# Block transposes on VectorE and a way through DRAM in place of TensorE's transposes, in an LSH attention with an FFN

## The chip, the core and the metric

The program runs on one core of one Trainium2 chip. The metric is the device time of one execution in microseconds. "Before" was run three times. TensorE (PE in the profile, its weight loads PEld), VectorE (DVE), ScalarE (ACT) and GpSimd (POOL) work each through a queue of their own, in order; SyncE (SP) only issues DMAs.

## The reference

```
scores = q @ k.T / sqrt(64)                      # 4 batches, 8 heads, 768 rows, head size 64
scores = where(bucket(q) == bucket(k), scores, -1e9)    # buckets: signs of 6 projections
attn   = softmax(scores);   x = attn @ v         # to 3072 tokens of 512
h = x @ w_in;   g = h * clip(h + 3, 0, 6) / 6;   out = g @ w_out    # 512 -> 2048 -> 512
```

## The kernel before

Attention runs in 192 tiles: 32 heads (4 batches of 8) of six tiles, each 128 queries by 768 keys. Index k or g counts tiles, i heads. Products are float32 in two float32r parts, a rounded high part and a low part (the rest), so every matmul stands two or three times with parts of its operands.

For one tile: `scores` writes the scores (minus sign and bucket penalty included) into PSUM tile s; `lowest` (L340, DVE) copies them to the SBUF tile p and takes the row minimum; `exponential` (L352, ACT) makes p the probabilities, in place, and adds up the row. The values product needs keys on the partitions, and p has queries there; so `transp` (L362) transposes p by TensorE against the identity, six blocks of 128x128 into two PSUM tiles pt of three blocks. `split_p` copies each pt to its high part ph (L385, ACT) and puts the rest into pl (L386, DVE). `values` multiplies two tiles at once, in two halves of three key blocks; `output` (L427) takes the sum to SBUF, and DMAs bring it to a DRAM tile xs, a second part by an adding DMA from POOL.

The FFN (`ffn`) goes through 12 chunks of 256 tokens (three for each batch), 16 steps each. A step is `gemm1` (12 matmuls of 256 columns into h), `gate` (relu L514 on ACT, the product L515 on DVE, high part gh L519, low part gl L520) and, one step later, `gemm2` (six matmuls of 512 columns into po). The chunks of batch 0 run by themselves between tiles 52 and 53 (`first_ffn`). Those of batches 1 to 3 follow the attention by one batch: the generator `fill` is advanced twice a tile, so that from tile 106 on one FFN step stands beside every attention tile. When attention ends, 58 steps are left and run alone.

The order on PE, DVE, ACT and POOL is that of the program text. The main loop's round k issues the transposes of tile k, the exponential of k+1, the minimum of k+2, the scores of k+3 (LA), and the split of k. DMAs on SP are put in order by the framework; SP too works in order, and a DMA that waits holds up those behind it. `lead` also prepares the next head: a load, the cast L275, DMAs of parts, and on POOL scaling and splits (L249, L281, L283), and, once in six tiles, `hash_qk` on TensorE and `bits` (L301) on DVE.

Buffers that matter here: p two, the gate's gh and gl two each, g one, a tag "ob" with two of 4 KB for a chunk's inputs and outputs, pt two under each of two names. GF = 2 * 48 + FS is the tile from which the round takes its FFN form.

## Time and profile before

| what | value |
|---|---|
| median of three runs (range) | 1031.67 us (1030.36 to 1032.12) |
| the profiled execution | 1030.6 us, span 1028.8 us, granted clock 0.999 |
| TensorE busy, 600 to 700 us | 99.63 us of 100 |
| transposes L362 on PE | 1152 instructions |
| L386 pl<-pt,ph on DVE | 376, mean 550 ns |
| L385 ph<-pt on ACT | 376, mean 481 ns |
| DMA | 80.69 MB, mean 78 GB/s |

Busy times of one engine come from the profiler's records; matmuls overlap, so a group's mean is longer than the step from one start to the next. "Idle before" names what the engine waited for last. The chain follows the work that ended last back through what released it. A stretch's row gives the busy time of each engine within it.

### The profile page before, as it was taken

Reading aid. Unit: us, or ns where it says so; the run is one execution under the profiler, and the core shown is the slowest. Engines: PE = TensorE matmul, PEld = TensorE weight load, DVE = VectorE, ACT = ScalarE, POOL = GpSimd, SP = SyncE. Lnnn points to the kernel's source line nnn. Section 1 sums busy time; section 2 is a strip of 40 time slices with the busy share of each in tenths; the row PEclk is TensorE's granted clock in tenths of the full one; section 3 lists DMA queues with packets and bytes.
Section 4 is the critical chain, followed back from the end, with each engine's and each line's share of the span. In section 5 each row is a group of like instructions: output and inputs, shape, how many; then the busy total and the mean of one; then the engine's idle time right before and its main releaser. Section 6 shows DMA issues by size and latency. Waiting matters only on the chain.

```text
span 1028.8 us, 19009 instructions
## 1 busy us (share of the span) xinstructions
PE 1006.9 (98%) x6846; PEld 924.3 (90%) x6846; DVE 687.9 (67%) x1446; ACT 585.3 (57%) x1311; POOL 473.1 (46%) x535
## 2 busy tenths in 40 slices
PE   8999999999999999999999999999999999999997
PEld 7999878888999998898999999999899999899996
DVE  7999988998489998756555666665656553333332
ACT  6889865555488886554645554555454452333332
POOL 6777725666367775544544534543544232200100
PEclk9999999999999999999999999999999999999999
DMA  4567679000145555222321322321231011101000
GB/s 124 139 146 181 155 228 333 2 1 1 41 128 122 114 118 138 64 63 53 100 56 26 85 76 51 76 68 38 63 101 38 20 32 29 42 1 42 1 22 20
DMA packets 47413, 80.69 MB, mean 78 GB/s; under 512 B 5924, under 2 KB 27812, under 8 KB 47320
## 3 DMA queue, kind: packets, MB, share of 16 engines
q1 hardware_dynamic: 42840, 73.98, 24.8%
q0 software_dynamic: 4480, 5.51, 4.8%
q8 instruction: 54, 0.88, 0.4%
q14 instruction: 39, 0.32, 0.1%
HBM read 41.95 MB, written 18.09 MB: 58 GB/s over the span
## 4 chain that ended last, share of the span: by engine, by line
PE 80%; DVE 11%; ACT 4%; issue 3%; POOL 1%; DMA 1%; SPq 0%; DVEq 0%; POOLq 0%; ACTq 0%
PE pt L362 10%; PE h L506 7%; PE h L505 7%; PE h L507 7%; PE po L527 7%; PE po L529 7%; PE po L528 7%; PE acc L399 6%; PE acc L400 6%; PE s L330 5%; PE s L333 5%; DVE pl L386 2%; DVE p L340 2%; PE z L292 1%; DVE wr L192 1%
## 5 line engine op out<-in xcount | busy, mean ns | idle before, releaser
L340 DVE TENSOR_SCALAR_CACHE_REDUCE p<-s 128x768 f32<-128x768 f32 x192 | 183.4, 955 | 98.8 <-PE pt L362 95.0
L386 DVE TENSOR_TENSOR pl<-pt,ph 128x384 fp32r<-128x384 f32 x376 | 191.7, 550 | 50.2 <-ACT ph L385 48.2
L385 ACT CAST ph<-pt 128x384 fp32r<-128x384 f32 x376 | 165.5, 481 | 53.6 <-PE pt L362 43.1
L352 ACT ACTIVATE p<-p,m 128x768 f32<-128x768 f32 x192 | 179.5, 935 | 7.0 <-DVE p L340 6.5
L514 ACT ACTIVATE g<-h,three 128x256 f32<-128x256 f32 x192 | 91.5, 476 | 152.8 <-PE h L507 131.5
L520 POOL TENSOR_TENSOR gl<-g,gh 128x256 fp32r<-128x256 f32 x96 | 74.3, 774 | 204.2 <-DVE gh L519 160.6
L362 PE MATMUL pt<-ident,p 128*128 128x128 f32 x1152 | 160.4, 273 | 5.2 <-DVE pl L386 3.3
L362 PEld LDWEIGHTS pt<-ident,p 128*128 128x128 f32 x1152 | 135.8, 140 | 23.5 <-PE pt L362 3.9
L515 DVE SCALAR_TENSOR_TENSOR g<-g,h 128x256 f32<-128x256 f32 x192 | 80.5, 420 | 113.8 <-ACT g L514 111.3
L399 PE MATMUL acc<-ph,vv 128*128 128x256 f32 x564 | 152.2, 302 | 4.0 <-DVE pl L386 4.0
L505 PE MATMUL h<-xh,w 128*128 128x256 f32 x512 | 147.7, 289 | 1.2 <-ACT y L427 1.2
L506 PE MATMUL h<-xl,w 128*128 128x256 f32 x512 | 143.3, 280 | 0.4 <-DVE xl L497 0.4
L507 PE MATMUL h<-xh,w 128*128 128x256 f32 x512 | 143.2, 280 | 0.0
L400 PE MATMUL acc<-pl,vv 128*128 128x256 f32 x564 | 140.6, 282 | 0.0
L527 PE MATMUL po<-w,gh 128*128 128x512 f32 x320 | 126.7, 396 | 0.1
L529 PE MATMUL po<-w,gl 128*128 128x512 f32 x320 | 126.6, 396 | 0.0
L528 PE MATMUL po<-w,gh 128*128 128x512 f32 x320 | 126.1, 394 | 0.0
L399 PEld LDWEIGHTS acc<-ph,vv 128*128 128x128 f32 x564 | 107.0, 190 | 7.2 <-DVE pl L386 2.1
L400 PEld LDWEIGHTS acc<-pl,vv 128*128 128x128 f32 x564 | 107.4, 190 | 0.0
L330 PE MATMUL s<-kk,qq 76*128 76x384 f32 x384 | 100.9, 343 | 2.0 <-ACT kk L306 1.5
L505 PEld LDWEIGHTS h<-xh,w 128*128 128x128 f32 x512 | 96.4, 188 | 3.8 <-ACT y L427 2.4
L333 PE MATMUL s<-kk,qq 128*128 128x384 f32 x384 | 99.8, 341 | 0.0
(136 smaller groups left out, 2022.6 us busy)
## 6 DMA issues: line engine op xcount, KB each, us to landing
raw<-in_qkT SPq DMA_DIRECT2D x32, 384.0 KB, 3.5
kk<-qq SPq DMA_DIRECT2D x62, 192.0 KB, 3.2
wr<-in_w_in SPq DMA_DIRECT2D x16, 512.0 KB, 11.1
wr<-in_w_out SPq DMA_DIRECT2D x16, 512.0 KB, 3.9
vr<-in_v SPq DMA_DIRECT2D x32, 192.0 KB, 2.6
qq<-qq SPq DMA_DIRECT2D x31, 192.0 KB, 3.1
out<-ob SPq DMA_DIRECT2D x11, 512.0 KB, 2.7
xr<-xs SPq DMA_DIRECT2D x9, 512.0 KB, 3.7
```

What stands on the lines that cost most here:

```text
L340: nc.vector.tensor_scalar(out=pr_[:], in0=s[:, :, :HW], scalar1=CAP, scalar2=None, op0=ALU.min, op1=ALU.min, accum_out=m[:],)
L352: nc.scalar.activation(pr_[:], pr_[:], AF.Exp, bias=m[:], scale=-1.0, accum_out=sms[b][:, t, h : h + 1])
L362: nc.tensor.transpose(pt[:, x], probs[g][0][:, c, x * P : (x + 1) * P], ident[:])
L386: nc.vector.tensor_sub(lo[:, :, w], pt[:], hi[:, :, w].bitcast(F32))
L399: nc.tensor.matmul(acc[:], lhsT=vv[:, kt], rhs=hi[:, x], start=(kt == 0), stop=False)
L400: nc.tensor.matmul(acc[:], lhsT=vv[:, kt], rhs=lo[:, x], start=False, stop=(kt == KT - 1))
L505: nc.tensor.matmul(hp[:], lhsT=wi[:, 0, wc], rhs=xh, start=(cc == 0), stop=False)
L506: nc.tensor.matmul(hp[:], lhsT=wi[:, 0, wc], rhs=xl, start=False, stop=False)
L507: nc.tensor.matmul(hp[:], lhsT=wi[:, 1, wc], rhs=xh, start=False, stop=(cc == NCC - 1))
L527: nc.tensor.matmul(po[u], lhsT=gh[:, us], rhs=wo[:, 0], start=(fc == 0), stop=False)
L528: nc.tensor.matmul(po[u], lhsT=gh[:, us], rhs=wo[:, 1], start=False, stop=False)
L529: nc.tensor.matmul(po[u], lhsT=gl[:, us], rhs=wo[:, 0], start=False, stop=(fc == NFC - 1))
```

## The change

From tile 106 on (GT = 2 * 48 + FS + FT with FS = 8, FT = 2) TensorE transposes nothing. `flip` transposes p on VectorE, each block of 32x32 for itself, into a tile f, which SP writes to a DRAM tile fd. `move` reads it back in four DMAs of 32 partitions x 4 x 192 numbers each, so that every 32x32 block comes to the partitions of its keys; the two targets (spare and px) take turns. `split_p` reads the target two rounds later (LT = 2). To make the blocks land so, the scores of these tiles take their keys in another order (`half`). The second half's sub goes from DVE to POOL, and the gate's gh beside the FFN from DVE to ACT. A new function `beside_ffn` writes the round from tile 105 on, with 194 rounds in place of 192. Tiles f share the two p buffers. The "ob" buffers become "oa" and "ob", of which "ob" is spare's later; gh and gl become one tile, in "ga" and "gb" in turn, and "gb" alone while px holds "ga". POOL's long instructions for a head come in two halves from head 19 on (`spans`). FS goes from 4 to 8, so the FFN beside attention starts some tiles later.

The diff, without the parts that only rename tiles or hand buffers on:

```
@@ -28,7 +28,9 @@
-FS = 4
+FS = 8
+FT = 2
+LT = 2
...
@@ -216,11 +227,15 @@
     GF = 2 * HK + FS
+    GT = GF + FT
...
@@ -240,7 +255,7 @@
-        n = 4 if i <= 2 else 1
+        n = 4 if i <= 2 else 2 if i > GF // KT + 1 else 1
...
@@ -325,12 +340,17 @@
         k1, k2, q1, q2 = state[i]
         us = slice(t * P, (t + 1) * P)
         s = scs[g] = pair(f"s{g}")
+        def half(x, c: int):
+            if g < GT:
+                return x[:, c * HW : (c + 1) * HW]
+
+            x = x.rearrange("p (x g b) -> p g x b", x=KT, g=4)
+            return x[:, 2 * c : 2 * c + 2]
+
         for c in range(2):
-            cs_ = slice(c * HW, (c + 1) * HW)
-            nc.tensor.matmul(s[:, c, :HW], lhsT=q1[:KM, us], rhs=k1[:KM, cs_], start=True, stop=False)
+            nc.tensor.matmul(s[:, c, :HW], lhsT=q1[:KM, us], rhs=half(k1[:KM], c), start=True, stop=False)
         for c in range(2):
-            cs_ = slice(c * HW, (c + 1) * HW)
-            nc.tensor.matmul(s[:, c, :HW], lhsT=q2[:, us], rhs=k2[:, cs_], start=False, stop=True)
+            nc.tensor.matmul(s[:, c, :HW], lhsT=q2[:, us], rhs=half(k2, c), start=False, stop=True)
 
     def lowest(g: int):
 
...
@@ -362,6 +382,33 @@
             nc.tensor.transpose(pt[:, x], probs[g][0][:, c, x * P : (x + 1) * P], ident[:])
         if c:
             del probs[g]
+
+
+
+    written, moved, homes = {}, {}, []
+
+    def flip(g: int):
+        nonlocal written
+        x = sp.tile([P, S], F32, name=f"f{g}", tag="p", bufs=2)
+        nc.vector.transpose(x[:], probs.pop(g)[0][:].rearrange("p c k -> p (c k)"))
+        d = dp.tile([P, S], F32, name=f"fd{g}", tag="fd", bufs=4)
+        dma(out=d[:], in_=x[:])
+        written[g] = d, last
+
+    def move(g: int):
+        if not homes:
+            px = sp.tile([P, S], F32, name="px", tag="ga", bufs=1)
+            homes.extend([spare[0][:, :S], px[:]])
+        to = moved[g] = homes[g % 2]
+        d, _ = written.pop(g)
+        after = written[g + 1][1] if g + 1 in written else last
+        with tc.issue_after(after.ins):
+            for x in range(4):
+                r = slice(32 * x, 32 * x + 32)
+                dma(
+                    out=to[r].rearrange("b (i c) -> b i c", i=4),
+                    in_=d[:].rearrange("(i b) (g c) -> g b i c", i=4, g=4)[x],
+                )
 
     lent = []
 
...
@@ -380,10 +427,24 @@
                     for x in ("ph", "pl")
                 ]
             parts[u, c] = [x.rearrange("p (x w q) -> p x w q", x=QT, w=2) for x in both]
-        hi, lo = parts[u, c]
-        pt = pts.pop((g, c))
-        nc.scalar.copy(hi[:, :, w], pt[:])
-        nc.vector.tensor_sub(lo[:, :, w], pt[:], hi[:, :, w].bitcast(F32))
+        hi, lo = (x[:, :, w] for x in parts[u, c])
+        engine = nc.vector
+        if g < GT:
+            pt = pts.pop((g, c))[:]
+        else:
+            pt = moved[g].rearrange("p (i x a) -> p x i a", i=4, x=KT)[:, c * QT : (c + 1) * QT]
+            hi, lo = (x.rearrange("p x (i a) -> p x i a", i=4) for x in (hi, lo))
+            if c:
+                engine = nc.gpsimd
+        nc.scalar.copy(hi, pt)
+        lows.append(lambda: engine.tensor_sub(lo, pt, hi.bitcast(F32)))
+
+    lows = []
+
+    def split_lows():
+        for f in lows:
+            f()
+        lows.clear()
 
     accs = {}
     vdone = 0
...
@@ -507,17 +570,28 @@
+    g_turn = 0
+    def gate_tiles(n: str):
+        nonlocal g_turn
+        g_turn += 1
+        if homes or g_turn % 2:
+            x = sp.tile([P, 2, TC], F32R, name=f"gb{n}", tag="gb", bufs=1)
+        else:
+            x = sp.tile([P, 3, TC], F32R, name=f"ga{n}", tag="ga", bufs=1)
+        return x[:, 0], x[:, 1]
     def gate(n: str, fc: int, hp, copy, engine, between=lambda: None):
         g = sp.tile([P, TC], F32, name=f"g{n}_{fc}", tag="g", bufs=1)
-        gh = sp.tile([P, TC], F32R, name=f"gh{n}_{fc}", tag="gh")
-        gl = sp.tile([P, TC], F32R, name=f"gl{n}_{fc}", tag="gl")
+        gh, gl = gate_tiles(f"{n}_{fc}")
         nc.scalar.activation(g[:], hp[:], AF.Relu, bias=three[:], scale=1.0)
         nc.vector.scalar_tensor_tensor(
             out=g[:], in0=g[:], scalar=6.0, in1=hp[:], op0=ALU.min, op1=ALU.mult
         )
         between()
-        copy(gh[:], g[:])
-        engine.tensor_sub(gl[:], g[:], gh[:].bitcast(F32))
+        copy(gh, g[:])
+        engine.tensor_sub(gl, g[:], gh.bitcast(F32))
         return gh, gl
 
     def gemm2(fc: int, po, gh, gl):
...
@@ -804,7 +880,7 @@
-            copy, engine = (nc.scalar.copy, nc.vector) if b == B - 1 else (nc.vector.tensor_copy, nc.gpsimd)
+            copy, engine = nc.scalar.copy, nc.vector if b == B - 1 else nc.gpsimd
...
@@ -892,7 +968,47 @@
             ahead(0, x)
         for _ in range(2):
             cv(0)
-        for k in range(NS):
+        def beside_ffn(k: int):
+
+            for c in range(2):
+                if k < GT:
+                    transp(k, c)
+            whole = False
+            for _ in range(1 if k < GT else 2):
+                u = vnext // 2
+                if u < NS // 2 and (k < GT or k % 2 == 0 and k >= 2 * u + 2 + (LT if 2 * u >= GT else 0)):
+                    whole = value_half()
+            if k + 1 < NS:
+                exponential(k + 1)
+            late = k if k < GT else k - LT
+            if GT <= late < NS or k < GT:
+                for c in range(2):
+                    split_p(late, c, False)
+            next(fill, None)
+            if whole:
+                output(vnext // 2 - 1)
+            if k == NS + LT - 1:
+                homes.clear()
+            if k + 1 < NS:
+                flip(k + 1)
+            if k + 2 < NS:
+                lowest(k + 2)
+            split_lows()
+            if GT <= k < NS:
+                move(k)
+            if k + LA < NS and (k + LA) % KT == 2 and (k + LA) // KT + 1 < NJ:
+                hash_qk((k + LA) // KT + 1)
+                bits((k + LA) // KT + 1)
+            next(fill, None)
+            if k + LA < NS:
+                lead(k + LA)
+            else:
+                add()
+
+        for k in range(NS + LT):
+            if k >= GT - 1:
+                beside_ffn(k)
+                continue
             end = GB if k < GB else NS
             i, t = divmod(k, KT)
             if k == HK - XE:
```

What the change does to the order, at three places. First VectorE in one tile beside the FFN (step 6 of chunk 1), up to the next tile's first row: p is the scores' copy, pl_0 and pl_1 the two low halves, g the gate's product, gh its high part. Before:

```order
L340 TENSOR_SCALAR p_7146,m_7145<-s_7113 128x768
L386 TENSOR_TENSOR pl_0_7182<-pt_0_7136,ph_0_7181 128x3x128
L386 TENSOR_TENSOR pl_1_7186<-pt_1_7140,ph_1_7185 128x3x128
L515 SCALAR_TENSOR_TENSOR g_1_6_7195<-g_1_6_7195,h_1_6_7161 128x256
L519 CAST gh_1_6_7196<-g_1_6_7195 128x256
L340 TENSOR_SCALAR p_7212,m_7211<-s_7176 128x768
```

And now (f is the transposed tile, spare and px the two targets of the moves):

```order
L393 STREAM_TRANSPOSE f_7231<-p_7157 128x768
L360 TENSOR_SCALAR p_7236,m_7235<-s_7191 128x768
L440 TENSOR_TENSOR pl_0_7211<-spare,ph_0_7210 128x3x128
L589 SCALAR_TENSOR_TENSOR g_1_6_7250<-g_1_6_7250,h_1_6_7216 128x256
L393 STREAM_TRANSPOSE f_7279<-p_7236 128x768
```

The second sub and the cast gh are gone from this queue; the block transpose stands ahead of the minimum, behind the product of the step before.

Second, ScalarE at the same place, from one exponential (out p) to the next; y is the values' sum. Before:

```order
L352 ACTIVATE p_7097,sms_5328<-p_7097,m_7096 128x768
L427 COPY y_0_7174<-acc_7148 128x256
L385 CAST ph_0_7181<-pt_0_7136 128x3x128
L385 CAST ph_1_7185<-pt_1_7140 128x3x128
L514 ACTIVATE g_1_6_7195<-h_1_6_7161,three 128x256
L352 ACTIVATE p_7146,sms_5328<-p_7146,m_7145 128x768
```

And now, with gb the gate's one buffer:

```order
L372 ACTIVATE p_7157,sms_5278<-p_7157,m_7156 128x768
L439 CAST ph_0_7210<-spare 128x3x128
L439 CAST ph_1_7213<-spare 128x3x128
L488 COPY y_0_7103<-acc_7196 128x256
L588 ACTIVATE g_1_6_7250<-h_1_6_7216,three 128x256
L593 CAST gb_1_6_7251<-g_1_6_7250 128x256
L372 ACTIVATE p_7236,sms_5278<-p_7236,m_7235 128x768
```

The casts read SBUF instead of PSUM, and the gate's cast has come between the relu and the next exponential.

Third, where the new rounds begin on VectorE: from round 106 to round 109, rt being the transposed reciprocals that scale the first chunk xr.

```order
L529 TENSOR_TENSOR xr_0_5538<-xr_0_5538,rt_0_0_5690 128x256
L393 STREAM_TRANSPOSE f_5697<-p_5657 128x768
L360 TENSOR_SCALAR p_5702,m_5701<-s_5671 128x768
L529 TENSOR_TENSOR xr_0_5538<-xr_0_5538,rt_0_1_5717 128x256
L393 STREAM_TRANSPOSE f_5722<-p_5702 128x768
L360 TENSOR_SCALAR p_5727,m_5726<-s_5711 128x768
L316 TENSOR_SCALAR qq_5662<-z_5733,thr,val 44x768
L529 TENSOR_TENSOR xr_0_5538<-xr_0_5538,rt_0_2_5759 128x256
L393 STREAM_TRANSPOSE f_5764<-p_5727 128x768
L360 TENSOR_SCALAR p_5769,m_5768<-s_5747 128x768
L440 TENSOR_TENSOR pl_0_5754<-spare,ph_0_5753 128x3x128
L529 TENSOR_TENSOR xr_0_5538<-xr_0_5538,rt_0_3_5787 128x256
```

Each of these rounds scales one of the chunk's four parts beside a block transpose and a minimum; the first product of the FFN (L589) stands only behind this piece, in round 110. On SP each tile adds the write of f and four moves. Two tiles of it, with the parts of the next head between:

```order
L78 DMA fd_5699<-f_5697 128x768
L78 DMA spare<-fd_5654 32x4x192 x4
L78 DMA raw_5745<-in_qkT 128x768
L78 DMA fd_5724<-f_5722 128x768
L78 DMA px<-fd_5699 32x4x192 x4
L78 DMA kk_5661<-qq_5662 12x768
L78 DMA vr_5777<-in_v 128x384
L78 DMA fd_5766<-f_5764 128x768
L78 DMA spare<-fd_5724 32x4x192 x4
```

The write of a tile stands ahead of the moves of the tile before it, and the next head's DMAs take their places between.

More of the change, by code (lines that the diff above doesn't have):

```diff
@@ L912, in lsh_attention_moe @@
                 pair_turn = 0
-            third = k < GF + 2
+            third = True
             whole = False
-            for _ in range(1 if third and k != HK else (2, 0)[k % 2]):
+            for _ in range(1 if k != HK else 2):
                 if vnext < k - k % 2:
@@ L940, in lsh_attention_moe @@
                 next(fill, None)
-            if k + LA >= NS:
-                add()
             if k < GB:
```

35 lines of the change are left out of this document (25 added, 10 removed).

## Prediction

> **What bounds the kernel now.** The page comes first: its engine line, and the chain that ended last.
>
> ```profile
> span 1028.8 us, 19009 instructions
> PE 1006.9 (98%) x6846; PEld 924.3 (90%) x6846; DVE 687.9 (67%) x1446; ACT 585.3 (57%) x1311; POOL 473.1 (46%) x535
> PE 80%; DVE 11%; ACT 4%; issue 3%; POOL 1%; DMA 1%; SPq 0%; DVEq 0%; POOLq 0%; ACTq 0%
> ```
>
> TensorE is busy 98% and carries 80% of the chain. An average hides stages, so the second view is the busy time by stretches: first the stage that the change rewrites (attention beside the FFN), then the tail with the FFN alone.
>
> ```profile
> 500.00:600.00 100.00, 99.76 (x687) 92.51 (x686) 61.30 (x130) 53.52 (x122) 48.01 (x48) 1.00 0.29 71
> 900.00:1000.00 100.00, 100.00 (x652) 90.37 (x651) 35.01 (x87) 36.32 (x83) 6.33 (x12) 1.00 0.05 17
> ```
>
> The columns are length, PE, PEld, DVE, ACT, POOL, granted clock, DMA share, GB/s. In both stretches TensorE has no gap and a full clock, so there a TensorE instruction costs what it takes from the next one's start. The third view is the window from the first transpose of tile 106 to the last of tile 191, for the transposes' line alone; then one tile's six transposes in the chain, and two starts of the FFN's second product.
>
> ```profile
> 413.40:851.90 438.50, 70.25 (x516) 61.12 (x516) 1.00 0.25 60
> 413.52 0.49 PE L362 MATMUL pt<-ident,p 128*128 128x128 f32 x3
> 851.27 0.82 PE L362 MATMUL pt<-ident,p 128*128 128x128 f32 x6
> 693.12 0.65 PE pt L362 x6
> 949.66 0.39 PE L527 MATMUL po<-w,gh 128*128 128x512 f32 x1
> 952.45 0.39 PE L527 MATMUL po<-w,gh 128*128 128x512 f32 x1
> ```
>
> 516 transposes are 86 tiles of six. Tiles 106 and 191 start 437.75 us apart, 85 steps, so **5.15 us a tile**, and 0.65 of that are transposes. An FFN step alone takes 952.45 - 949.66 = 2.79 us. The profiled execution then reads: tile 106 at 413.5, 86 tiles to 856.4, 58 FFN steps alone (161.8), 10.6 of edges, end at 1028.8.
>
> **The change part by part.** GT is 106, so all 516 transposes of this window go; 516 / 6 x 0.65 = 56 us of TensorE. If nothing else ended later, a tile would take 5.15 - 0.65 = 4.50 us. No other engine is full by its sum. DVE had 61.3% of 5.15 = 3.16 us a tile; it loses a sub and the gate's cast and gains the block transpose. POOL had 2.47 and gains a sub; ACT had 2.76 and gains the gate's cast. These are the rows:
>
> ```profile
> L340 DVE TENSOR_SCALAR_CACHE_REDUCE p<-s 128x768 f32<-128x768 f32 x192 | 183.4, 955 | 98.8 <-PE pt L362 95.0 <-PE s L333 1.9
> L301 DVE TENSOR_SCALAR qq<-z,thr,val 44x768 fp32r<-44x768 f32 x31 | 33.7, 1086 | 8.8 <-PE z L292 7.0 <-issue 1.2
> L262 DVE CAST qq<-raw 64x768 fp32r<-64x768 f32 x1 | 0.6, 557 | 2.2 <-DMA raw<-in_qkT 2.2
> L515 DVE SCALAR_TENSOR_TENSOR g<-g,h 128x256 f32<-128x256 f32 x192 | 80.5, 420 | 113.8 <-ACT g L514 111.3
> L519 DVE CAST gh<-g 128x256 fp32r<-128x256 f32 x96 | 37.2, 388 | 3.8
> L317 POOL TENSOR_TENSOR vv<-vr,vv 128x384 fp32r<-128x384 f32 x32 | 32.3, 1010 | 2.6
> ```
>
> The block transpose reads and writes 768 columns in SBUF and appears nowhere before. The rows of 768 columns bound it: 0.56 (L262) and 1.09 us (L301). I take 0.955, the row of the minimum (L340), since two of the three rows lie there. The Trainium skill (Vector Engine (DVE) Microarchitecture Reference, section 3.8) says that the transpose path sustains one element per cycle per lane; with the 0.96 GHz that it states, my estimate would be 0.80 us and the end some 12 us earlier; no run here shows it yet. POOL's new sub of 128x384 is priced by L317, same size and operands: 1.01 us. So DVE comes to 3.16 - 0.55 - 0.39 + 0.96 = 3.2 us, POOL to 3.5, ACT to 3.2, all under 4.5.
>
> What binds instead is a **ring through ACT and DVE**, read from the rows of the order shown above. In one tile ACT runs exponential, two casts, relu, the gate's cast gh, then the next exponential. DVE runs flip (after the exponential), minimum, sub, the gate's product, and only then gh may run. Before, the exponential only fed TensorE a tile later, and gh stood on DVE behind its product, so no such ring closed. Its pieces:
>
> ```profile
> 701.24 0.93 ACT L352 ACTIVATE p<-p,m 128x768 f32<-128x768 f32 x1
> 702.07 0.19 ACT L352 ACTIVATION_READ_ACCUMULATOR p<-p,m 128x1 f32 x1
> 699.41 0.96 DVE L340 TENSOR_SCALAR_CACHE_REDUCE p<-s 128x768 f32<-128x768 f32 x1 [1.44 <-PE pt L362]
> 700.29 1.02 DVE L386 TENSOR_TENSOR pl<-pt,ph 128x384 fp32r<-128x384 f32 x2
> 201.25 0.41 DVE L515 SCALAR_TENSOR_TENSOR g<-g,h 128x256 f32<-128x256 f32 x1
> 201.69 0.41 ACT L519 CAST gh<-g 128x256 fp32r<-128x256 f32 x1 [1.00 <-DVE g L515]
> 202.00 0.67 ACT L188 ACTIVATE wr<-wr 128x512 f32<-128x512 f32 x1
> ```
>
> Exponential to the end of its accumulator read: 702.26 - 701.24 = 1.02. Handing over costs 0.03 (201.66 to 201.69); I count 0.05 ahead of flip. Flip 0.955 and 0.03. Minimum to the next start 0.88, sub 0.51 (two in 1.02), product 0.42 and 0.03, gh 0.31 to the next start on ACT. Sum **4.21 us**. Four things stand in the ring now and then: the hash bits once in six tiles (L301 above), the cast of the next head, and at a chunk's end four casts and two output scalings:
>
> ```profile
> L275 ACT CAST qq<-raw 128x768 fp32r<-128x768 f32 x13 | 10.7, 824 | 0.0
> L496 ACT CAST xh<-xr 128x256 fp32r<-128x256 f32 x31 | 10.7, 404 | 3.3 <-DVE xr L466 3.3
> L543 ACT ACTIVATE ob<-po 128x512 f32<-128x512 f32 x18 | 9.8, 596 | 9.0 <-PE po L529 9.0
> ```
>
> 1.09/6 + 0.82/6 + 4 x 0.40/16 + 2 x 0.60/16 = 0.18 + 0.14 + 0.10 + 0.08 = 0.50, so 4.71 us.
>
> One wait is new. The sub read PSUM and SBUF before; now both inputs lie in SBUF. Such a sub on DVE, and POOL at the same time:
>
> ```profile
> 580.23 1.29 DVE L497 TENSOR_TENSOR xl<-xr,xh 128x256 fp32r<-128x256 f32 x2
> 580.49 0.75 POOL L520 TENSOR_TENSOR gl<-g,gh 128x256 fp32r<-128x256 f32 x1 [3.81 <-DVE gh L519]
> 415.13 1.84 POOL L283 TENSOR_TENSOR qq<-raw,qq 64x768 fp32r<-64x768 f32 x1
> 415.81 2.31 DVE L497 TENSOR_TENSOR xl<-xr,xh 128x256 fp32r<-128x256 f32 x2
> L497 DVE TENSOR_TENSOR qq<-xr,kk 128x256 fp32r<-128x256 f32 x4 | 1.7, 425 | 1.9 <-ACT kk L496 1.9
> ```
>
> Two such subs take 0.85 beside an idle POOL (the 425 ns row), 1.29 and 2.31 here: 0.4 and 1.5 us of waiting, ending with POOL's instruction. The change halves POOL's long instructions from head 19 on (spans), so the wait is near the smaller. POOL's own new sub starts as its cast ends, 1.0 before DVE's, and is about over. That leaves tiles in which POOL has a head's split, scaling or values to do, three in six; I take the 0.4 for these, **0.2 a tile**, and keep 0 and 0.5 as ends. The Trainium skill (SBUF — State Buffer, Who interferes with whom) states that a VectorE instruction with two SBUF inputs and a GpSimd instruction that reads SBUF exclude each other for a whole instruction; the trace agrees, with the 2.31 us row, and what it would do here in full is the third rival below. So the ring takes 4.71 + 0.2 = **4.9 us**, past TensorE's 4.50.
>
> The rest of the change hides, if its cover holds. A tile adds 768 KB to the queues (first row: 160 to 175 us, queues full; the last row is from there too):
>
> ```profile
> DMA packets 3513, 5.70 MB, mean 380 GB/s; under 512 B 190, under 2 KB 2687, under 8 KB 3512
> raw<-in_qkT SPq DMA_DIRECT2D x32, 384.0 KB, 3.5
> out<-ob SPq DMA_DIRECT2D x11, 512.0 KB, 2.7
> 627.00 0.59 SPq L76 DMA_DIRECT2D qq<-qq  x1
> xs<-y SPq DMA_DIRECT2D x1, 128.0 KB, 8.9
> ```
>
> At the 380 GB/s of 160 to 175 us that is 2.1 us, with 0.29 x 5.15 = 1.5 from before 3.6 of 4.9. SP issues five more, at most 5 x 0.59 = 3.0 us. The write must land before the next flip, which reuses its source: 0.96 + 0.1 + landing, 2.7 to 3.5 by the two rows, so 3.8 to 4.6, below 4.9. The moves' data is asked for two tiles after they are issued; POOL's split, 1.0, is needed a tile later. Behind a flip that waits stand the minimum, the sub and the product, and the next scores on TensorE wait for the minimum. The single gate buffer makes gh wait for the second product of the step before, done a little after half a tile on TensorE. The permuted keys read by the scores are priced at nothing, ends 0 and 0.1 us a tile; TensorE has 0.4 spare.
>
> The sum. Four tiles (106 to 109) now run before the first FFN step, as the order's third place shows, at the write's 3.9 us: 15.6. 81 tiles follow at 4.9 (396.9); three more steps carry FFN and values only (2.79 + 0.72, say 3.5: 10.5); the last values 1.4; 60 FFN steps alone (167.4); the same edges 10.6. From 413.5: 413.5 + 15.6 + 396.9 + 10.5 + 1.4 + 167.4 + 10.6 = **1015.9 us**, against 1028.8. The profiled execution took 1.8 us beyond its span, and the median shown, 1031.67, lies 1.1 above it: about **1018**. Each 0.1 us a tile is 8.1 us, and the break-even ring is 4.9 + 12.9/81 = 5.06 us.
>
> **Rivals.** *First: TensorE still sets the pace*, at 4.50 us a tile: 32.4 us less, 986. For it: TensorE had no gap before. Against it: flip would have to cost 0.56 instead of 0.955 and POOL never be met. *Second: the write's landing is the new ring.* It decides from 5.06 - 1.06 = 4.0 us; at 4.5 a tile takes 5.56 and the kernel 1071. For it: 8.9 us for 128 KB while the queues were full (the last of the rows on transfers). Against: the queues come to about 73%. *Third, on the slower side: VectorE's sub waits for POOL.* POOL is at work 3.5 of 4.9 us; met at a random point with an instruction of 1.01 left half, 0.7 x 0.5 = 0.36 more than none, that is 5.07 us, no change; with the halved scalings and splits queued back to back, about 0.55, 5.26, **1047**. It decides from a mean wait of 0.35 us. For it: 1.5 us at 415.81. Against: POOL's sub should end as DVE's begins. That transposes remain is excluded by the code: transp runs for k < GT alone.
>
> **How the numbers follow.** Forecast (ring 4.75 to 5.03, 1006 to 1029): 0.52. TensorE's pace: 0.12. POOL's lock: 0.22, of which 0.08 without visible change. The write: 0.10. Something unseen, slower: 0.04. A measurement of this kernel tells 0.2%, 2 us, from no change. Faster: 0.52 - 0.03 at its upper edge + 0.12 = 0.61; same 0.08 + 0.03 = 0.11; slower 0.28. The range runs from 1000, short of the first rival, to 1046, which takes in nearly all of the third and cuts most of the second.
>
> **What would show it.** Tiles 110 to 190 at 4.9 us, TensorE near 92% there with gaps ahead of scores or of the second product, and the chain of waits passing through ACT and DVE. Flip at 0.955. The sub with two SBUF inputs over 0.55 on average, worst beside POOL's halved splits. SP never waiting 1 us for the write. If flip waits on a DMA, the second rival is right; if TensorE stays over 98%, the first. A flip of 1.6 us would alone add 50 us and make the prediction wrong.

## The result, and the profile after

The kernel with the change takes **1092.79 us** (median of 4 runs, 1084.93 to 1094.53), the kernel before 1031.89 beside it (4 runs). The ratio is 1.0574, 95% interval 1.0519 to 1.0629: slower by 61 us. The forecast was 1018, faster, and its range ended at 1046.

The page of the changed kernel, its engine line and the engines of the chain that ended last:

```profile
span 1091.3 us, 19386 instructions
PE 994.0 (91%) x6330; PEld 894.3 (82%) x6330; DVE 707.4 (65%) x1350; ACT 623.6 (57%) x1407; POOL 567.9 (52%) x662
PE 56%; DVE 12%; DMA 9%; issue 7%; POOL 7%; ACT 6%; SPq 2%; DVEq 0%; POOLq 0%; ACTq 0%
```

TensorE was busy 98% and is busy 91%; its share of the chain fell from 80% to 56%, and DMA, POOL and "issue", 1 to 3% each before, grew to 7 to 9%. So TensorE waits, and for several things, not one. The first and the last flip in VectorE's timeline say where the time lies:

```profile
410.94 0.98 DVE L393 STREAM_TRANSPOSE f<-p 128x768 f32<-128x768 f32 x1 [0.31 <-PE pt L382]
899.79 0.98 DVE L393 STREAM_TRANSPOSE f<-p 128x768 f32<-128x768 f32 x1
```

86 flips are 85 steps: 488.85 / 85 = **5.75 us a tile**, where the forecast had 4.9 (and four tiles at 3.9, so 4.85 on average) and the kernel before 5.15. From the last flip to the end are 191.5 us, much as the forecast's terms behind the tiles. The whole error is in the tile's time: 85 x 0.9 = 76 us. The stretch with full tiles, by engine (length, PE, PEld, DVE, ACT, POOL, granted clock, DMA share, GB/s):

```profile
420.00:860.00 440.00, 367.00 (x2149) 323.18 (x2150) 259.67 (x424) 223.75 (x521) 256.96 (x292) 0.92 0.65 190
```

TensorE is busy 367 / 440 = 83% here, not 92%: 4.80 us of each tile, and idle 0.95. The forecast had 4.50 and 0.4. So 0.3 us a tile are busy time that grew, beside a granted clock of 0.92 in place of 1.00, and the rest is more waiting. Five of the rows that say what it and the others wait for, in the same stretch (total us, times, longest):

```profile
ACT gb L593 <- PE po L603: 61.9, 17, 7.9
PE z L305 <- DVE p L360: 34.8, 11, 7.1
DVE f L393 <- DMA fd<-f: 27.8, 11, 5.7
PE s L351 <- DVE p L360: 25.0, 19, 3.2
DVE qq L316 <- PE z L307: 17.1, 11, 1.9
```

Two of these are new kinds, and a third has grown. Flips wait for a write (third row). The hash z waits for a tile's minimum (second row), for both use the one pair of PSUM banks; TensorE is idle for 73 us in this stretch, and nearly half of that is this wait. The gate's cast waits for the second product (first row), which stands behind z on TensorE while its input holds the one gate buffer; before, the gate waited 16.6 us for that product in the same stretch, on GpSimd. The worst place shows them joined, in the timelines of SyncE, VectorE and TensorE:

```profile
723.97 0.38 SPq L78 DMA_DIRECT2D xr<-xs  x1
727.70 0.61 SPq L78 DMA_DIRECT2D kk<-qq  x1
732.45 0.34 SPq L78 DMA_DIRECT2D fd<-f  x1
```

```profile
726.67 0.98 DVE L393 STREAM_TRANSPOSE f<-p 128x768 f32<-128x768 f32 x1 [2.47 <-DMA fd<-f]
736.07 0.98 DVE L393 STREAM_TRANSPOSE f<-p 128x768 f32<-128x768 f32 x1 [5.71 <-DMA fd<-f]
737.17 0.96 DVE L360 TENSOR_SCALAR_CACHE_REDUCE p<-s 128x768 f32<-128x768 f32 x1
```

```profile
730.90 0.28 PE L570 MATMUL h<-xh,w 128*128 128x256 f32 x1
738.28 0.63 PE L305 MATMUL z<-qq,pjl 128*108 128x384 f32 x1 [7.10 <-DVE p L360]
```

The flip that began at 726.67 was done at 727.65, but its write went out at 732.45, and SP issued nothing from 728.31 on. SyncE's own waits name the cause: it stood 4.1 us for the load xr of 723.97 to land. The trace's issues show why. They signal through eight DMA semaphores in turn, and the write, the eighth issue behind that load, takes the same semaphore. In the whole stretch this wait comes twice, 4.8 us together. The next flip needs that tile's buffer and waits 5.7 us; the minimum stands behind it; z needs the minimum's PSUM pair, and TensorE stands 7.1 us with the second product and the next scores queued behind z. The groups of the flip and of VectorE's sub over the whole run, with shapes kept apart:

```profile
L393 DVE STREAM_TRANSPOSE f<-p 128x768 f32<-128x768 f32 x86 | 84.0, 977 | 126.3 <-ACT p L372 85.0 <-DMA fd<-f 31.6 <-ACT ph L439 6.7
L440 DVE TENSOR_TENSOR pl<-spare,ph 128x384 fp32r<-128x384 f32 x43 | 45.5, 1059 | 0.0
L440 DVE TENSOR_TENSOR pl<-px,ph 128x384 fp32r<-128x384 f32 x43 | 24.2, 564 | 3.4 <-ACT ph L439 3.4
```

The flip's 0.977 was forecast as 0.955. The sub takes 0.56 on odd tiles and 1.06 on even ones.

### The profile page after: what moved, and what is told of

Same layout as the page of the kernel before. It is cut to its first block, busy times and chain, and to the rows that moved or that the text cites. A ratio compares the mean times of both kernels' runs of the same rounds, so it can differ in the third digit from the quotient of the medians.

```text
span 1091.3 us, 19386 instructions
## 1 busy us (share of the span) xinstructions
PE 994.0 (91%) x6330; PEld 894.3 (82%) x6330; DVE 707.4 (65%) x1350; ACT 623.6 (57%) x1407; POOL 567.9 (52%) x662
## 4 chain that ended last, share of the span: by engine, by line
PE 56%; DVE 12%; DMA 9%; issue 7%; POOL 7%; ACT 6%; SPq 2%; DVEq 0%; POOLq 0%; ACTq 0%
PE pt L382 5%; PE h L569 5%; PE acc L460 5%; PE h L570 5%; PE h L568 5%; PE po L601 5%; PE po L603 5%; PE po L602 4%; PE acc L461 4%; PE s L351 4%; DMA spare<-fd 4%; PE s L353 4%; DVE pl L440 3%; DVE p L360 2%; POOL qq L298 2%
## 5 line engine op out<-in xcount | busy, mean ns | idle before, releaser
L372 ACT ACTIVATE p<-p,m 128x768 f32<-128x768 f32 x192 | 179.8, 936 | 18.3 <-DVE p L360 17.7
L593 ACT CAST gb<-g 128x256 fp32r<-128x256 f32 x137 | 55.7, 407 | 213.5 <-DVE g L589 136.2
L393 DVE STREAM_TRANSPOSE f<-p 128x768 f32<-128x768 f32 x86 | 84.0, 977 | 126.3 <-ACT p L372 85.0
L594 POOL TENSOR_TENSOR gb<-g,gb 128x256 fp32r<-128x256 f32 x89 | 65.5, 736 | 172.0 <-ACT gb L593 170.1
L589 DVE SCALAR_TENSOR_TENSOR g<-g,h 128x256 f32<-128x256 f32 x192 | 80.0, 417 | 108.6 <-ACT g L588 108.0
L351 PE MATMUL s<-kk,qq 76*128 76x384 f32 x384 | 108.1, 363 | 27.3 <-DVE p L360 25.3
L439 ACT CAST ph<-pt 128x384 fp32r<-128x384 f32 x204 | 91.4, 473 | 26.7 <-PE pt L382 15.8
L440 DVE TENSOR_TENSOR pl<-pt,ph 128x384 fp32r<-128x384 f32 x204 | 104.0, 550 | 2.5 <-ACT ph L439 1.9
L353 PE MATMUL s<-kk,qq 128*128 128x384 f32 x384 | 103.3, 351 | 0.0
L351 PEld LDWEIGHTS s<-kk,qq 76*128 76x128 f32 x384 | 65.2, 197 | 46.4 <-DVE p L360 28.0
L601 PE MATMUL po<-w,gb 128*128 128x512 f32 x242 | 100.3, 414 | 3.0 <-ACT ob L617 2.0
L569 PEld LDWEIGHTS h<-xl,w 128*128 128x128 f32 x512 | 97.9, 191 | 3.1 <-DVE xl L560 0.6
```

Of the source, the lines that this page charges most:

```text
L351: nc.tensor.matmul(s[:, c, :HW], lhsT=q1[:KM, us], rhs=half(k1[:KM], c), start=True, stop=False)
L353: nc.tensor.matmul(s[:, c, :HW], lhsT=q2[:, us], rhs=half(k2, c), start=False, stop=True)
L372: nc.scalar.activation(pr_[:], pr_[:], AF.Exp, bias=m[:], scale=-1.0, accum_out=sms[b][:, t, h : h + 1])
L439: nc.scalar.copy(hi, pt)
L440: lows.append(lambda: engine.tensor_sub(lo, pt, hi.bitcast(F32)))
L569: nc.tensor.matmul(hp[:], lhsT=wi[:, 0, wc], rhs=xl, start=False, stop=False)
```

## The experiments

Each kernel is the changed one with the edit shown. Ratios are to the kernel before, timed beside it; "against 1092.8" means the changed kernel's median. Steps from flip to flip are worked out, as above, from the flips' starts in VectorE's timeline.

**First: which part.** The flip path is undone (e_rest), or parts of the way through DRAM are left out.

```
e_rest       -FT = 2                            +FT = 88      # GT = 192: no tile is flipped
             -for k in range(NS + LT):          +for k in range(NS):
             -if k >= GT - 1:                   +if k >= GT:
             -third = True                      +third = k < GF + 2
             -range(1 if k != HK else 2)        +range(1 if third and k != HK else (2, 0)[k % 2])
e_flip_only  -dma(out=d[:], in_=x[:])  and in move() no DMAs;  +for x in homes: nc.vector.memset(x, 0.01)
e_write      in move() no DMAs;  +for x in homes: nc.vector.memset(x, 0.01)
e_moves      the write only for the first tile; all moves read that tile of DRAM
```

> Undoes the flip path alone: every tile keeps TensorE's six transposes, and no tile is flipped, written or moved. What stays of the change: one wide buffer (oa), gate buffers that alternate, the gate's cast on ScalarE, the finer POOL splits, eight in place of four steps before the FFN starts. All theories that put the loss into the flip, the write and the moves expect 1025 to 1045 (as before, some us for four more tiles without FFN). 1060 or more would put the loss into the rest of the change.

> The flip stays, the write and the four moves are left out; the casts read two targets that were filled once, so the values are those of a constant. Theory A (the transfers and their one queue stretch the ring): the ring of ScalarE and VectorE runs at the forecast 4.9 us a tile or less, 1010 to 1025. Theory B (the ring of ScalarE and VectorE is itself longer than was counted, the lock of VectorE and GpSimd included): 5.5 us a tile or more, 1070 to 1095. Theory C (once in six tiles the hash stands on TensorE ahead of the second product, behind a minimum of the same PSUM pair, and the one gate buffer closes a ring through TensorE): about half of the loss stays, 1040 to 1070.

> Flip and write stay, the four moves are left out (casts read the two constant targets). Theory A in its form 'moves wait for POOL at the head of SP's queue and the next write stands behind them': the write goes out at once, 1010 to 1030. Theory A in its form 'a write's landing of 3.5 us holds the buffer that the next flip needs': 1075 or more. Theories B and C as for the flip alone.

> Flip and moves stay, but the moves read one constant tile in DRAM that is written once, so no tile is written. If the moves' wait for POOL hurts only through the write behind it: 1020 to 1040. If the moves' traffic itself (384 KB a tile, the FFN's load of 512 KB landing in 8.4 us beside it) delays casts and loads: 1050 or more.

| run | median us | ratio, 95% interval |
|---|---|---|
| e_rest | 1033.38 | 1.0018 (1.0008 to 1.0027) |
| e_flip_only | 1071.35 | 1.0381 (1.0354 to 1.0409) |
| e_write | 1073.84 | 1.0422 (1.0405 to 1.0439) |
| e_moves | 1066.41 | 1.035 (1.0319 to 1.0382) |

The loss is the flip path's: without it the rest of the change costs 2 us. But two thirds of it stay with no transfer at all. Theory A alone has fallen; it keeps about 20 us, and those come only where write and moves run together: e_write is 2.5 us above the flip alone, e_moves is not above it at all (its moves read a tile that is written once, so they wait for no write). The flip alone, at 1071, lies where the ranges of theories B and C meet, and its steps show a part of both. They fall into kinds by their place in the head: 4.3 to 5.1 us for most, 6.5 for the tile with the hash, 6.2 for the tile three later (the profiled execution was the fastest of the four, 1065.9). From VectorE's timeline, with rows between left out:

```profile
650.13 0.98 DVE L393 STREAM_TRANSPOSE f<-p 128x768 f32<-128x768 f32 x1 [1.46 <-ACT p L372]
652.12 0.55 DVE L431 TENSOR_TENSOR pl<-px,ph 128x384 fp32r<-128x384 f32 x1
653.65 1.09 DVE L316 TENSOR_SCALAR qq<-z,thr,val 44x768 fp32r<-44x768 f32 x1 [0.99 <-PE z L307]
654.77 0.42 DVE L580 SCALAR_TENSOR_TENSOR g<-g,h 128x256 f32<-128x256 f32 x1
656.65 0.98 DVE L393 STREAM_TRANSPOSE f<-p 128x768 f32<-128x768 f32 x1 [1.46 <-ACT p L372]
...
661.39 0.98 DVE L393 STREAM_TRANSPOSE f<-p 128x768 f32<-128x768 f32 x1 [1.63 <-ACT p L372]
665.72 0.98 DVE L393 STREAM_TRANSPOSE f<-p 128x768 f32<-128x768 f32 x1 [1.46 <-ACT p L372]
667.70 2.51 DVE L431 TENSOR_TENSOR pl<-spare,ph 128x384 fp32r<-128x384 f32 x1
672.00 0.98 DVE L393 STREAM_TRANSPOSE f<-p 128x768 f32<-128x768 f32 x1 [1.09 <-ACT p L372]
```

A bare step, 661.39 to 665.72, takes 4.33: the ring of the forecast (4.21), 0.12 longer. The hash's step, 650.13 to 656.65, is 6.52: sub, then 0.99 of waiting for z, 1.09 of bits, and only then the gate's product, whose cast the next exponential waits for. The step from 665.72 is 6.28 because the sub takes 2.51. TensorE and GpSimd at these two places:

```profile
652.34 0.40 PE L305 MATMUL z<-qq,pjl 128*108 128x384 f32 x1 [2.19 <-DVE p L360]
```

```profile
666.18 2.63 POOL L264 TENSOR_SCALAR raw<-raw 64x384 f32<-64x384 f32 x2
668.47 1.32 POOL L431 TENSOR_TENSOR pl<-spare,ph 128x384 fp32r<-128x384 f32 x1
```

z could start only when the minimum was done, 2.19 us after TensorE was free for it. And GpSimd scales the next head's queries, two halves back to back, while VectorE's sub with two SBUF inputs is due; behind the scaling stands GpSimd's own sub. VectorE's sub, begun at 667.70, ends at 670.21, 0.42 after that one (669.79).

**Second: the two long steps, and the write's queue**, each alone and all three together.

```
e_hash   hash_qk(..); bits(..) behind the second next(fill, None) of beside_ffn, not ahead of it
e_scale  -nc.gpsimd.tensor_scalar_mul(raws[i][:D, c], raws[i][:D, c], -SCALE)
         +nc.scalar.mul(raws[i][:D], raws[i][:D], -SCALE)       # behind the two casts of split_p
e_actw   -dma(out=d[:], in_=x[:])   +nc.scalar.dma_start(out=d[:], in_=x[:])
e_all    the three edits
```

> Everything of the change stays; once in six tiles the hash and its bits stand behind the second product and the gate, not ahead of them. With the flip alone the tile that carries the hash takes 6.5 us from flip to flip against 4.5 of a bare one, and VectorE stands 1.0 us for z and 1.1 in the bits ahead of the gate's product. If that is a part of the ring, most of those 2.1 us go, in 14 heads: 1062 to 1075. If the hash only finds another place in the same ring (the next flip or scores wait for the bits instead): 1085 to 1095.

> Everything of the change stays; the scaling of the next head's queries (L264, two instructions of 1.4 us on GpSimd, once in six tiles) is done by ScalarE, behind the casts, where it waits for the gate's product anyway. Lock theory: VectorE's subtraction takes 2.5 us in place of 0.55 while GpSimd scales, and the tile that meets it takes 6.2 us: 14 heads times 1.6 us, less what the scaling costs on ScalarE, 1068 to 1080. If the long subtraction has another cause, or GpSimd's lateness is paid elsewhere: 1085 to 1097.

> Everything of the change stays; the write of a flipped tile is issued by ScalarE's queue (behind the casts), the moves stay on SP's queue. If the 20 us by which the change is slower than the flip alone come from the write standing behind moves that wait for GpSimd: 1070 to 1080. If the writes wait for a transfer that holds their semaphore slot, or the transfers land later because they share the 16 engines: 1088 to 1100 (ScalarE then waits itself).

> The three edits together: hash behind the gate, scaling on ScalarE, write from ScalarE's queue. If the three losses are terms of one sum: 1092 less 20 to 28, less 15 to 22, less 15 to 20, so 1022 to 1042. If they are one wait seen three times: 1065 or more.

| run | median us | ratio, 95% interval |
|---|---|---|
| e_hash | 1084.62 | 1.0515 (1.05 to 1.0531) |
| e_scale | 1078.09 | 1.0467 (1.0432 to 1.0501) |
| e_actw | 1087.52 | 1.0549 (1.0523 to 1.0575) |
| e_all | 1067.11 | 1.036 (1.0328 to 1.0391) |

The lock is there: with the scaling on ScalarE the sub from spare, 1059 ns in the group above, is

```profile
L444 DVE TENSOR_TENSOR pl<-spare,ph 128x384 fp32r<-128x384 f32 x43 | 29.7, 692 | 0.0
```

and 15 us are gained, by the medians, where 13 to 25 were expected. That the Trainium skill (SBUF — State Buffer, Who interferes with whom) lets the loser wait for a whole instruction agrees with the 2.51 us; here the sub waited for the rest of the scaling and for GpSimd's own sub as well. The other two are misses: e_hash gains 8, not 18 to 31, and e_actw 5, where 13 to 23 were expected, with an interval that overlaps the changed kernel's. The three together gain 26, nearly their sum of 28, so they are not one wait seen three times, but this is far from the 50 to 71 that were expected. In e_hash the wait moved: TensorE's scores now wait for the bits, in their single PSUM pair. "PE s L351 <- DVE qq L316" comes to 18.3 us there, in 12 waits. So it is the pair, not the order alone; and that the write stands behind moves on SP's queue costs little, or ScalarE's queue pays as much.

**Third: the pair itself; and is the rest a ring of ScalarE and VectorE, or TensorE?**

```
e_zbank  z = [bank([P, HW], ..) for j in range(2)]  in place of  z = pair(..), for the heads beside the FFN;
         bits in two instructions, one a bank
f_clean  e_flip_only, with the edits of e_scale, e_zbank and e_hash
f_pool   f_clean, and  engine = nc.gpsimd  for both halves of split_p
e_all2   the change, with the edits of e_scale, e_zbank, e_hash and e_actw
```

> Everything of the change stays, and the hash keeps its place ahead of the second product; but z goes to two single PSUM banks that the transposes left free, so that it waits for no minimum (and the scores behind it wait for no bits). TensorE waits 35 us for the minimum ahead of z in this stage. If those stalls are lost for good, since TensorE needs 4.5 us of each tile and cannot catch up: 1055 to 1070. If the ring of ScalarE and VectorE sets the pace and z only waits because TensorE is early: 1085 to 1097.

> No write and no moves (casts read constant targets), as in the kernel with the flip alone; and the scaling on ScalarE, z in banks of its own, the hash behind the gate. If hash and lock are what made the flip alone cost 5.44 us a tile: about 4.8 to 4.9, which is 1010 to 1025, the time that was forecast. If something else keeps the pair of ScalarE and VectorE or TensorE at this pace: 1045 to 1070.

> As the run before, and GpSimd takes both subtractions of a flipped tile, so VectorE's bare ring is 0.55 us shorter (about 3.8 us) and no instruction of VectorE there can wait for GpSimd. If the ring of ScalarE and VectorE still sets the pace: 20 to 45 us faster than the run before. If TensorE's own work and stalls set it: within 10 us of it. If GpSimd (two subtractions, the gate's and the split of the next head, about 4.0 us a tile) becomes the bound: slower than it.

> The whole change with write and moves, the write from ScalarE's queue, the scaling on ScalarE, z in banks of its own and the hash behind the gate. Against the kernel with the first three edits (1067): if the hash's hold on TensorE is worth what its waits for minimum and bits show there (26 us of TensorE): 1035 to 1050. If the transfers now set the pace (flips waited 37 us for a write there): 1060 to 1070.

| run | median us | ratio, 95% interval |
|---|---|---|
| e_zbank | 1070.38 | 1.0378 (1.036 to 1.0397) |
| f_clean | 1023.71 | 0.9935 (0.9916 to 0.9954) |
| f_pool | 1022.26 | 0.9918 (0.9898 to 0.9937) |
| e_all2 | 1043.53 | 1.0108 (1.0079 to 1.0137) |

Two free PSUM banks for z are worth 22 us, somewhat under the 23 to 38 expected. z's 34.8 us of waiting are gone there, but TensorE's scores wait 40.1 us for the minimum in the stretch, 15 more than in the change. With hash and lock out of the way and no transfers, the forecast's time comes out (f_clean, expected 1010 to 1025): 4.95 us a tile. And the ring of ScalarE and VectorE is not what sets the rest: f_pool takes a sub off VectorE's ring, whose bare step falls from 4.33 to 3.9 us, and gains 1.4 us. The stretches, of the flip alone, of f_clean and of f_pool:

```profile
420.00:860.00 440.00, 381.62 (x2311) 335.69 (x2312) 281.11 (x458) 238.22 (x556) 269.93 (x310) 0.96 0.22 55
```

```profile
420.00:860.00 440.00, 409.04 (x2567) 364.16 (x2566) 280.06 (x499) 268.28 (x618) 259.93 (x306) 0.98 0.24 59
```

```profile
420.00:860.00 440.00, 407.88 (x2581) 366.34 (x2579) 238.17 (x412) 273.21 (x619) 339.38 (x393) 0.98 0.24 59
```

TensorE is busy 93% in both of the last, 4.6 us a tile. A bare ring of 4.33 is shorter than that mean, so TensorE has next to nothing to spare in the short steps, and what it loses in the step with the hash it cannot well win back. This is argued from the means. f_pool does not prove it alone, since GpSimd, busy 59% of the stretch in f_clean, is busy 77% there and may take back a part of what VectorE gains.

**Fourth: why do transfers that were counted as hidden still cost 20 us?** (1043.5 against 1023.7.) The flipped tile's buffer is taken away: VectorE transposes p in place. Both p buffers then hold probabilities, and the write reads one of them.

```
e_inpl   -nc.vector.transpose(x[:], probs.pop(g)[0][:].rearrange("p c k -> p (c k)"))
         +x = probs.pop(g)[0][:].rearrange("p c k -> p (c k)");  nc.vector.transpose(x, x)
f_write  f_clean with the write (ScalarE's queue);   f_moves  f_clean with the moves from one tile of DRAM
e_all3   e_all2 with the flip in place
```

> Everything of the change stays, but VectorE flips a tile in place: no buffer of its own for the flipped tile, so the flip waits for no write; instead the minimum two tiles later waits for the write that leaves this buffer. In the change flips wait 32 us in all for the write before. If that buffer closes a ring of its own (flip 1.0, issue, landing 3.5, about 5 us): those waits go, 1076 to 1085. If the minimum then waits as long: 1088 to 1098.

> As the run without write and moves that took 1023.7 (scaling on ScalarE, z in banks of its own, hash behind the gate), and the write is there again, from ScalarE's queue; no moves. If the 20 us between that run and the whole change with the same edits (1043.5) come from the buffer that a flipped tile holds until its write has landed: 1032 to 1040. If they come only where moves and writes meet: 1022 to 1028.

> As that run of 1023.7, with the moves (from one constant tile in DRAM), no writes. If casts and GpSimd wait for moves that land late: 1030 to 1040. If moves alone are hidden: 1022 to 1028.

> The whole change with scaling on ScalarE, z in banks of its own, hash behind the gate, write from ScalarE's queue, and the flip in place. Against 1043.5 with a buffer of its own: if the buffer's ring is the rest of the loss: 1025 to 1034, level with the kernel before. If the rest is the moves' or the casts' wait for data: 1038 to 1046.

| run | median us | ratio, 95% interval |
|---|---|---|
| e_inpl | 1057.01 | 1.027 (1.0239 to 1.0301) |
| f_write | 1028.33 | 0.998 (0.9969 to 0.9991) |
| f_moves | 1023.96 | 0.9933 (0.9919 to 0.9946) |
| e_all3 | 1029.25 | 0.9982 (0.9967 to 0.9996) |

The buffer is the largest single term: against 1092.8 the flip in place gains 36 us (expected 8 to 17), and with the other edits it gains 14 of the 20 that were open. Write and moves hardly cost anything apart (5 and 0 us) and 20 together, where each move also waits for the write of its tile, as it does not in f_moves. The flip's groups in f_clean and in e_all2 hold just this difference, in the idle time ahead of the flip, 92.5 and 111.5 us (f_write has 97.7, f_moves 92.6, e_all3 96.2):

```profile
L406 DVE STREAM_TRANSPOSE f<-p 128x768 f32<-128x768 f32 x86 | 84.0, 977 | 92.5 <-ACT p L385 91.0 <-PE pt L395 0.3
```

```profile
L406 DVE STREAM_TRANSPOSE f<-p 128x768 f32<-128x768 f32 x86 | 84.1, 978 | 111.5 <-ACT p L385 71.2 <-DMA fd<-f 35.6 <-ACT ph L451 3.8
```

In a bare step the flip idles 1.46 us, for the exponential. A write stays hidden as long as it has landed by the start of the next flip, and in a bare step 0.98 of flip, 0.03 to its issue and 3.3 of landing make the 4.33. A flip that waited for a write shows when this landed. In f_write these 15 writes took 3.4 to 3.7 us from issue to the flip's start, one 4.2; in e_all2, beside the moves, 20 writes took 3.5 to 5.2, seven of them over 4.3. One such step of e_all2, VectorE and the issue on ScalarE's queue:

```profile
527.05 0.98 DVE L406 STREAM_TRANSPOSE f<-p 128x768 f32<-128x768 f32 x1 [1.46 <-ACT p L385]
533.10 0.98 DVE L406 STREAM_TRANSPOSE f<-p 128x768 f32<-128x768 f32 x1 [3.18 <-DMA fd<-f]
```

```profile
528.06 0.36 ACTq L408 DMA_DIRECT2D fd<-f  x1
```

In the changed kernel it is the same and more: of the 13 writes waited for, five were issued 0.7 to 1.0 us after the flip's end and one 4.8, and they took 3.0 to 5.3 us to land. The in-place flip does a second thing, which was not expected. VectorE in the changed kernel, and in e_inpl:

```profile
663.37 0.98 DVE L393 STREAM_TRANSPOSE f<-p 128x768 f32<-128x768 f32 x1 [1.89 <-ACT ph L439]
664.47 0.96 DVE L360 TENSOR_SCALAR_CACHE_REDUCE p<-s 128x768 f32<-128x768 f32 x1
```

```profile
662.30 0.98 DVE L393 STREAM_TRANSPOSE p<-p 128x768 f32<-128x768 f32 x1 [1.46 <-ACT p L372]
663.20 0.92 DVE L360 TENSOR_SCALAR_CACHE_REDUCE p<-s 128x768 f32<-128x768 f32 x1
```

The minimum starts 0.90 us behind the flip's start, not 1.10: before, it wrote the buffer that the flip was still reading; now it writes the other one. Its bare step is 4.09 us, not 4.33. Its flips idle 105.3 us in all, the change's 126.3, so 21 us less ahead of the flips; the earlier start can be worth at most 85 x 0.2 = 17. No run separates the two.

**Fifth: do the terms add, and does SP's order matter now?**

```
e_two    the change, with the edits of e_inpl and e_zbank
e_all4   e_all3 with the write on SP's queue again
```

> Everything of the change stays, with two buffers altered and no instruction moved to another engine or place: the flip in place, and z in two PSUM banks of its own. If the two losses are terms of a sum (36 us and 22 us, each measured alone against 1092.8): about 1035. If both edits free the same wait: 1048 or more.

> As the run of 1029.3 (scaling on ScalarE, z in banks of its own, hash behind the gate, flip in place), but the write is issued by SP's queue again, as in the change. If a write behind moves that wait for GpSimd on SP's queue still costs: 1032 to 1040. If the buffer was all that made its lateness count: 1026 to 1031, the same or faster, since ScalarE then waits for no flip.

| run | median us | ratio, 95% interval |
|---|---|---|
| e_two | 1048.46 | 1.0171 (1.0158 to 1.0185) |
| e_all4 | 1028.33 | 0.9976 (0.9964 to 0.9987) |

They overlap: 36 and 22 alone, 44 together, where a sum would have given 58. This fits the worst place above, where z waited for a minimum that stood behind a flip that waited for a write. The order on SP's queue costs nothing any more (e_all4 and e_all3 differ by 0.9 us). e_all4 is the whole change with four edits, and is faster than the kernel before by 0.24% (0.13 to 0.36). Its stretch, and its flips' waits for the write, which now fall on the minimum:

```profile
420.00:860.00 440.00, 403.23 (x2531) 361.30 (x2531) 274.36 (x496) 265.95 (x615) 258.50 (x306) 0.98 0.72 211
```

```profile
DVE p L373 <- DMA fd<-p: 12.5, 11, 3.1
```

The median step in us by the tile's place in its head (tile number modulo six), and the mean of all 85:

```
place            0     1     2     3     4     5    mean
the change     7.84  4.93  4.33  6.20  5.06  5.20   5.75
e_flip_only    6.53  4.75  4.33  6.20  5.07  4.49   5.44
e_zbank        6.06  4.56  4.33  6.20  5.07  4.95   5.51
e_scale        7.75  4.99  4.45  4.82  5.07  5.21   5.67
e_inpl         6.51  4.84  4.09  5.84  4.83  4.48   5.34
f_clean        4.91  4.61  4.33  4.40  5.06  4.47   4.95
e_all4         4.91  5.20  4.10  4.40  4.83  4.47   5.01
```

Place 0 is the hash, place 3 the lock, place 4 the next head's cast (0.83, as forecast). Place 2 is bare. Each row is one execution; that of e_scale was the slowest of its four (1084.8).

## Why the prediction was wrong, by its own steps

Two steps failed: the cover of the write, and the hash bits priced without the wait ahead of them. A third term, the lock, was too small in the tile where it strikes. By the medians, the flip with none of the three takes 1023.7 us (f_clean); hash and lock put back add 48 (e_flip_only), and the transfers on top 21 (the change).

- **TensorE's 56 us, and the flip's price.** Right: the transposes are gone, f_clean's tile keeps TensorE busy for 4.6 us, and the flip takes 0.977. My estimate of 0.80 by the Trainium skill (Vector Engine (DVE) Microarchitecture Reference, section 3.8) was below it; the time from the flip's start to the next instruction's, 0.90 at best, is above it too.
- **The ring's pieces, 4.21.** Right to 0.12: a bare step is 4.33. But "four tiles at the write's 3.9: 15.6" took 18.1 (the first four steps), with two flips waiting for a write.
- **"The write must land before the next flip ... 3.8 to 4.6, below 4.9."** This step failed: flips waited 31.6 us for writes, 13 times. Taking the buffer away gained 36 us, the most of any single edit, though a part of that (at most 17) is the minimum's earlier start; counted from the other end, all transfers together cost 21 us on top of the flip alone. The median landing was in its range (3.5 of 2.7 to 3.5), so the yardstick was wrong twice. 4.9 is a mean of short and long steps, and the cycle has to fit into the short ones, 4.33; and it is the late landings, up to 5.3, and the late issues that a buffer without a second one makes the flip wait for, not the median. The second rival, "the write's landing is the new ring", was right in kind at 0.10, but its point of decision, 4.0 us, was taken against the mean too; it lay at 3.3.
- **Bits "once in six tiles", 0.18.** The cost counted was the instruction's. The wait in front of it was left out: z waits for a minimum through the one PSUM pair, the bits wait for z, and the gate's product and the second product stand behind them. This step failed too. That tile takes 6.5 us bare of transfers and 7.8 with them, against 4.9 in f_clean. Banks of its own for z gained 22 us.
- **The lock, 0.2 a tile.** Right in kind, and not far off in size: 15 us gained are 0.17 a tile, and place 3 falls by 1.8 us, 0.3 a tile, from e_flip_only to f_clean. But it comes as nearly 2 us in one tile of six (6.20 and 4.33), not as 0.4 in three. The prediction let GpSimd's own sub be over before VectorE's begins; behind the scaling it starts later, and VectorE's sub waits for both. The row at 415.81 showed it: only 1.16 of its 1.5 us of waiting lie beside L283, and GpSimd's next subs began at 417.05. The third rival alone would not have made the kernel slower (its 1047 needs 0.55).
- **"TensorE has 0.4 spare", and a tile as the larger of ring and TensorE.** This is what made three small errors large. The ring (4.33 in a bare step) and TensorE (4.5 by the forecast, 4.6 busy in f_clean) are nearly level and are tied by single buffers (the PSUM pair, the gate buffer, the flipped tile), so the long step of one is not well made up by the other; this last step is argued, not measured alone. The single gate buffer itself was not tried with a second one: gate casts waited 62 us for the second product, but 8.6 in e_zbank and 11.3 in e_hash with the buffer unchanged, so most of that wait came from z standing ahead of that product.
- **The moves, SP and the casts of data.** Right apart (f_moves costs 0.3 us; the order on SP was not told from nothing), wrong together: beside the moves single writes land up to 1.9 us past the 3.3 that are hidden.
- **The tail and the tiles without FFN.** Right: 191.5 us behind the last flip, 191.7 in f_clean.

What remains open: e_all4 is 4.6 us above f_clean, with minimums and casts that wait for transfers now and then; how the buffer's 36 us divide between the write and the earlier minimum; and what the shared DMA semaphores cost, since no run gave each transfer its own.

## What to carry to other kernels

Hold a buffer's cycle (write, hand over, land) against the shortest step that recurs, not against the mean: a mean hides exactly the steps in which there is no cover. When an operation is taken off the busiest engine, list the single buffers that tie that engine to its new neighbours; with two resources nearly level, much of each wait at such a buffer is lost for good. And ask of an occasional instruction what it waits for and who stands behind it, not only how long it runs.

## What the runs showed of the hardware

The granted clock falls behind gaps and then lengthens the work itself. In the change, by stretches of ten and twenty microseconds (the first lies where the new rounds begin without the FFN, and reads 0.66 in f_clean):

```profile
420.00:440.00 20.00, 13.44 (x54) 11.83 (x55) 12.13 (x21) 8.47 (x20) 8.42 (x10) 0.57 0.61 175
640.00:650.00 10.00, 8.51 (x55) 7.29 (x53) 4.21 (x8) 5.63 (x13) 5.77 (x6) 1.00 0.71 216
730.00:740.00 10.00, 2.90 (x17) 2.63 (x16) 2.77 (x6) 2.63 (x6) 3.44 (x4) 0.76 0.78 212
```

A mean busy share of 85%, with no gap over 0.5 us up to 649, kept 1.00; behind the gap of 7.1 us the clock is 0.76, and z's matmuls there take 0.53 us instead of the 0.34 that they take in the flip alone. The trace's clock records show what the means hide: between 400 and 900 us the clock is halved in twelve spells of 3.4, 6.8 or 17.1 us, 68 us together, against two spells and 17 us in f_clean. A gap of 7 us is not needed: in the 3.4 us ahead of the twelve spells TensorE was busy 0 to 43%, and the one of 17.1 us began in a gap of 2.8. Over the stretch the clock is 0.92 with the change and 0.98 in f_clean, and TensorE's busy time 4.80 and 4.60 us a tile: an estimate of 0.2 x 85 = 17 of the 61 us may be the clock's. This is a reading; no run isolated it. A load of 512 KB (xr) landed in 8.4 us by the median, against 3.7 before, and in 3.9 in e_all4, with the same transfers beside it:

```profile
xr<-xs SPq DMA_DIRECT2D x9, 512.0 KB, 8.4
```
